# A long convolution with a feed-forward layer: another order of issue, block 3's feed-forward part in halves, and loads moved to GpSimd

## The chip, the cores and the metric

One core of one Trainium2 chip. The metric is the time of one execution on the device in microseconds; several executions are measured and their median is given. A core has five engines with instruction streams of their own: TensorE (PE in the profile; its weight loads are shown apart as PEld), VectorE (DVE), ScalarE (ACT), GpSimd (POOL) and SyncE (SP). Transfers are issued by SP or by GpSimd and carried out by the core's 16 DMA engines.

## The reference

Two layers on a sequence of 2048 tokens with 640 features, in bfloat16: a gated long convolution, then a SwiGLU feed-forward part with 1728 inner features. Cut to what matters:

```python
def reference(q, k, v, shift_k, ssm_k, ssm_D, w_gate, w_up, w_down):
    x = q
    # A: short causal convolution of k (4 taps), times v, then a causal
    # convolution over the whole sequence with the filter ssm_k, by FFT
    k_shift = sum(k_pad[:, t:t+S] * shift_k[:, 3 - t] for t in range(4))
    kv = k_shift * v
    y = irfft(rfft(kv, 2*S) * rfft(ssm_k, 2*S))[:S] + kv * ssm_D
    h = x + layernorm(x) * y
    # B
    n = layernorm(h)
    return h + (silu(n @ w_gate) * (n @ w_up)) @ w_down
```

## The kernel before

The sequence is cut into four blocks of 512 tokens, a block into four rows of 128 tokens. Everything is done on blocks: the spectrum of a block of the filter (G0 to G3), of a block of kv (X0 to X3), products of spectra added up over the blocks so far (the *mac* of block j has j + 1 pairs), the inverse transform, the gating, and the feed-forward part of the block. A transform is matrix products with constant matrices, WF forward and WI back, with DVE sums and differences around them.

- Loads: `load_k` (L477), the filter blocks g (`load_g`, L289), v (`load_t`, L296), x (`load_x`, L301), WF (L903), WI (L909), the row of ssm_D (L904, "skip"), the weights gate and up in three pieces each (`load_weights`, L737, into `wgu`) and down (`load_wd`, L746 and L749, into `wd`).
- Of block 0, k and g are turned by PE transposes (L411, with their eviction in L413), the later blocks by transposing DMAs (L404). The four taps are a matrix product (L490); DVE multiplies by v (L513 for block 0, with the kv in L515 for the later ones). Nine matrix products on the identity (L882, `warm`) stand between.
- Forward transforms: L329 on PE, evicted in L319 or L322. The mac: L537, L542 and L545 on DVE, and L581 and L582 at its end. The first normalisation is `ln1` (L606 to L636; its power on GpSimd, L610). The inverse transform: L662 to L677 on DVE, L698 on PE, L707 and L709. `turn_h` (L722 on ACT or L724 on DVE) normalises h and transposes it to hT.
- `ffn`: gate and up projections (`proj`, L769) in seven groups of 256 inner features; silu in L783, then either a copy of up by ACT and a DVE product (L785, L787) or one DVE product straight from PSUM (L786). The last 192 features stand apart (`odd_chunks`, L809 to L811, with the weights in `wodd`). Down projection: L833 and L845. The result of blocks 0 to 2 is put on top of h, which `ffn` has stored (L754), by an adding transfer on GpSimd (L852); block 3 adds on DVE (L862, L864).

`LEAD` gives for a block how many groups of `ffn` are done in halves of 256 tokens (`HALVES`: the rows 1, 3 first, then 0, 2), with a `matmul` of 256 columns in place of 512; a group that is not is done whole, after them.

No scheduler works here. Each piece of work is recorded with the buffers it reads and writes (`Plan.add`) and gets a number; `Plan.run` then emits the pieces in the order of the table `ORDER`, and every engine runs its own in that sequence. A number written as its complement (-20 for piece 19) takes the piece in its other form:

```python
for i in ORDER:
    op = self.ops[max(i, ~i)]
    assert op.deps <= done
    if i < 0:
        op.fn = op.other[2]
```

The other form of a load is the same load issued by GpSimd instead of SP; of an addition in the mac (`added`, L243) an adding transfer issued by GpSimd instead of a DVE instruction; of an eviction the DVE instead of ACT; of `turn_h` the DVE instead of ACT; of the up copy the single DVE product:

```python
def load(nbytes, fn, w, r=()):
    return plan.add("sp", nbytes, lambda: fn(nc.sync), r, w, ("pq", nbytes, lambda: fn(nc.gpsimd)))
```

Large tiles share an arena of 22 units, handed out in the same order ("arena" in the profile).

Of the kernel before, what the change touches and what calls it, by code (L numbers as in the profile page):

```python
# [41 lines left out]
LEAD = {0: 6, 3: 2}  # L42
# [149 lines left out]
def kernel(ctx: ExitStack, tc: tile.TileContext, A_q, A_k, A_v, A_shift_k, A_ssm_k, A_ssm_D, B_x,  # L192
# [458 lines left out]
    def inverse(A, x, n1, j, pieces=WHOLE):  # L651
# [50 lines left out]
        stats = []  # L702
        for rs in HALVES if LEAD.get(j) else (ROWS,):
            s = new("sm")
# [46 lines left out]
    def ffn(j, hT, h, n1, end=False):  # L751
# [6 lines left out]

        lead = LEAD.get(j, 0)

# [230 lines left out]
```

## Time and profile before

| | before |
|---|---|
| median of three executions | 251.34 us (250.96 to 253.92) |
| span of the profiled execution (no other time is recorded for it) | 251.4 us |
| PE busy | 237.3 us (94%) |
| PEld busy | 153.0 us (61%) |
| DVE busy | 197.7 us (79%) |
| ACT busy | 173.9 us (69%) |
| POOL busy | 54.0 us (21%) |
| moved by the DMA engines | 33.66 MB |

Busy times are those of one profiled execution. Weight loads run beside matrix products, so PE and PEld are not to be added. L numbers are lines of the kernel. A group row has the line, engine, operation, output and input tiles with their shapes and the count; then busy time and mean duration in ns; then the idle time ahead of them and what ended it. A timeline row has the start, the length and then the same, with the idle time before it in brackets. A row of transfers gives their count, the size of one and the median time from issue to landing. "SPq" and "POOLq" are the queues of transfers that these engines issue.

### The profile page before, as it was taken

The page shows a single profiled execution, that of the slowest core. Times are in us where ns is not written, and L with a number is a line of the kernel's source. Part 1 is how long each engine was busy: PE and PEld are TensorE (multiplying, and loading weights), DVE is VectorE, ACT ScalarE, POOL GpSimd, SP SyncE. Part 2 cuts the span into 40 slices and gives each one's busy share as a digit, 9 for nine tenths or more (in the row PEclk, how much of TensorE's full clock was granted, in tenths as well). Part 3 has the DMA queues.
Part 4 walks back from the last instruction along what each step waited for, and adds up shares of the span by engine and source line. Part 5 has one row for each costly group of instructions (what it writes and reads, how often), then busy time and mean ns, then how long its engine had stood idle before and what let it go on. Part 6 is the DMA issues. An engine that isn't in the chain of part 4 may idle for free.

```text
span 251.4 us, 5138 instructions
## 1 busy us (share of the span) xinstructions
PE 237.3 (94%) x2113; PEld 153.0 (61%) x2125; DVE 197.7 (79%) x249; ACT 173.9 (69%) x300; POOL 54.0 (21%) x54
## 2 busy tenths in 40 slices
PE   3869997999999999999999999999999999999994
PEld 3447675788777677444465676454456785465662
DVE  2379999999999999999999989999999542131222
ACT  2449998999999976975988789983542865325100
POOL 0002003231540313220270404263612110000030
PEclk9999999999999999999999999999999999999999
DMA  5995699774998654685345468889592200000052
GB/s 156 376 212 163 127 324 352 231 197 92 165 246 292 202 81 81 105 154 133 79 66 146 86 99 194 148 146 163 98 224 29 26 0 3 0 0 3 0 78 78
DMA packets 37283, 33.66 MB, mean 134 GB/s; under 512 B 22470, under 2 KB 32076, under 8 KB 37260
## 3 DMA queue, kind: packets, MB, share of 16 engines
q1 hardware_dynamic: 31884, 21.38, 32.1%
q0 software_dynamic: 5376, 11.96, 25.9%
q8 instruction: 16, 0.26, 0.4%
q14 instruction: 7, 0.06, 0.1%
HBM read 16.29 MB, written 4.59 MB: 83 GB/s over the span
## 4 chain that ended last, share of the span: by engine, by line
PE 56%; ACT 17%; DMA 10%; DVE 9%; issue 4%; SPq 3%; DVEq 0%; ACTq 0%; POOLq 0%
PE ps L769 24%; PE ps L845 22%; ACT arena L319 7%; DMA arena<-in_A_ssm_k_dram 7%; PE ps L698 5%; DMA arena<-arena 3%; ACT sg L785 2%; PE ps L490 2%; SPq L404 2%; ACT junk L606 1%; PE ps L329 1%; PE ps L833 1%; DVE arena L674 1%; DVE arena L663 1%; DVE arena L662 1%
## 5 line engine op out<-in xcount | busy, mean ns | idle before, releaser
L769 PE MATMUL ps<-arena,wgu 128*128 128x512 bf16 (+1 forms) x668 | 116.7, 328 | 1.4 <-ACT sg L809 0.5
L769 PEld LDWEIGHTS <-wgu 128*128 128x128 bf16 x680 | 66.2, 98 | 45.3 <-issue 1.4
L845 PE MATMUL ps<-wd,tT 128*128 128x320 bf16 x416 | 59.1, 299 | 0.0
L845 PEld LDWEIGHTS <-tT 128*128 128x128 bf16 x416 | 39.8, 98 | 17.2 <-issue 1.8
L542 DVE TENSOR_TENSOR arena<-arena 128x2560 bf16<-128x2560 bf16 x30 | 44.1, 1484 | 0.2
L783 ACT ACTIVATE sg<-ps 128x1024 bf16<-128x1024 f32 (+1 forms) x28 | 26.9, 968 | 20.3 <-PE ps L769 19.7
L329 PE MATMUL ps<-arena,WF 128*128 128x320 bf16 x176 | 29.8, 299 | 1.2 <-ACT arena L319 0.9
L785 ACT CAST sg<-ps 128x1024 bf16<-128x1024 f32 (+1 forms) x23 | 23.0, 998 | 6.9 <-PE ps L769 3.1
L319 ACT CAST arena<-ps 128x320 bf16<-128x320 f32 (+1 forms) x48 | 25.2, 583 | 1.9 <-DVE arena L545 1.1
L610 POOL TENSOR_TENSOR sm<-sm,neghalf 128x4 f32<-128x4 f32 (+1 forms) x10 | 16.6, 1659 | 43.4 <-DVE sm L646 43.1
L787 DVE TENSOR_TENSOR tT<-sg,sg 128x1024 bf16<-128x1024 bf16 (+1 forms) x23 | 15.5, 673 | 11.5 <-ACT sg L785 11.5
L243 POOL DMA_DIRECT2D arena<-arena x11 | 13.3, 1211 | 47.4 <-DVE arena L542 11.2
L329 PEld LDWEIGHTS <-WF 128*128 128x128 bf16 x176 | 17.1, 98 | 10.0 <-issue 2.3
L606 ACT ACTIVATE junk<-arena 128x640 bf16<-128x640 bf16 x28 | 20.8, 744 | 1.3 <-DVE arena L709 1.3
L545 DVE TENSOR_TENSOR arena<-arena 128x2560 bf16<-128x2560 bf16 x14 | 20.7, 1487 | 0.2
L319 ACT ACTIVATE arena<-ps 128x640 bf16<-128x640 f32 (+1 forms) x32 | 20.2, 655 | 0.3
L698 PE MATMUL ps<-arena,WI 128*128 128x320 bf16 x96 | 15.7, 299 | 0.9 <-issue 0.6
L850 ACT ACTIVATE row<-ps,sm 128x640 bf16<-128x640 f32 x12 | 9.5, 791 | 8.2 <-PE ps L845 8.0
L709 DVE SCALAR_TENSOR_TENSOR arena<-arena,sm,ps 128x640 bf16<-128x640 bf16 x16 | 13.6, 876 | 1.8 <-ACT ps L707 1.8
L852 POOL DMA_DIRECT2D out_dram<-row x12 | 11.7, 1153 | 14.1 <-ACT row L850 14.1
L707 ACT ACTIVATE ps<-ps,sm 128x640 f32<-128x640 f32 x16 | 12.1, 770 | 3.7 <-PE ps L698 3.5
L698 PEld LDWEIGHTS <-WI 128*128 128x128 bf16 x96 | 9.0, 97 | 5.6 <-issue 1.3
(91 smaller groups left out, 240.8 us busy)
## 6 DMA issues: line engine op xcount, KB each, us to landing
arena<-arena POOLq DMA_DIRECT2D x11, 640.0 KB, 6.1
arena<-in_A_q_dram SPq DMA_DIRECT2D x4, 640.0 KB, 5.1
out_dram<-row POOLq DMA_DIRECT2D x13, 160.0 KB, 4.2
arena<-in_A_ssm_k_dram SPq DMA_DIRECT2D x3, 640.0 KB, 9.4
arena<-in_A_v_dram SPq DMA_DIRECT2D x3, 640.0 KB, 6.3
wd<-in_B_w_down_dram SPq DMA_DIRECT2D x2, 800.0 KB, 7.3
out_dram<-arena POOLq DMA_DIRECT2D x2, 640.0 KB, 5.8
wgu<-in_B_w_gate_dram SPq DMA_DIRECT2D x1, 800.0 KB, 6.5
```

What stands on the lines that cost most here:

```text
L319: (lambda: nc.scalar.activation(dst(), src(), ACT.Copy, scale=2.0)) if twice else (lambda: nc.scalar.copy(dst(), src())),
L329: nc.tensor.matmul(ap(ps)[:, h, 0:NH], w, ap(src)[:, r, h * NH:(h + 1) * NH], start=(first and i == 0), stop=(last and i == len(rs) - 1), ...
L542: dve(1402, lambda: v.tensor_mul(to(), X.part(xs), H.part(hs)), [X.at(xs), H.at(hs)], [at])
L545: added(1402 * n - 69 * (n - 1), lambda: v.tensor_add(to(), to(), b()), to, b, [what], at, n)
L606: act(725, lambda r=r: nc.scalar.activation(waste(), ap(x)[:, r, :], ACT.Square, scale=D ** -0.5, accum_out=sm(s, MSQ, (r,))), [(x, r)], [ ...
L610: nc.gpsimd.tensor_tensor(sm(s, RSTD, rs), sm(s, VAR, rs), ap(neghalf)[:, 0:len(rs)], op=ALU.pow)
L698: nc.tensor.matmul(ap(ps)[:, w, 0:NH], m, src[:, w * NH:(w + 1) * NH], start=(i == 0), stop=(i == len(terms) - 1))
L769: nc.tensor.matmul(split(ap(ps), n)[:, i, :], w(k), ap(hT)[:, k, lo:lo + n], start=(k == 0), stop=(k == KT - 1))
L783: act(905 if wide_ else 490, lambda: nc.scalar.activation(of(sg), of(*gate), ACT.Silu), [(gate[0], gate[1] + i) for i in range(m)] + (psu ...
L785: op = plan.add("act", 905 if wide_ else 490, lambda: nc.scalar.copy(of(co), of(*up)), psu + [sg], [co] + tt, ("dve", 1135 if wide_ else 6 ...
L787: op.rest = dve(602 if wide_ else 336, lambda: nc.vector.tensor_mul(to(), of(sg), of(co)), [sg, co], tt)
L845: nc.tensor.matmul(ap(ps[hf])[:, hf, 0:NH], ap(tT)[:, c * BLK + at:c * BLK + at + P], ap(wd)[:, c, hf * NH:(hf + 1) * NH], start=False, st ...
```

## The change

`LEAD` for block 3 goes from 2 to 4, and `ORDER` is another table; all else is the same. Of the table the pieces that take their other form differ: 24 loads and stores are issued by GpSimd in place of 5, 13 additions of the mac go as adding transfers in place of 11 (with the 12 of `ffn` 25 in place of 23), seven up copies are joined with the product in DVE in place of five, and seven `turn_h` are on DVE in place of six.

```diff
-LEAD = {0: 6, 3: 2}
+LEAD = {0: 6, 3: 4}
...
 ORDER = (
-    0, 1, 2, 3, 16, 18, -20, 5, 4, 8, 17, 186, 9, 20, 22, 7, 10, 11, -22, 24, -26, 23, 26, 75, 76, 13, 15, 12, 6,
...
+    -27, -187, 16, 1, 8, 2, 5, 0, 3, 20, 18, 21, 7, 9, 19, 10, 11, 17, -16, 24, 22, -24, 25, 75, 76, 77, 6, -13, 78,
...
```

SP's program began with these rows: k in two parts, the taps, then g1, v0, WF, skip, g0 and the rest (`in_A_ssm_k` is the filter g, `in_A_q` is x):

```order
L477 DMA arena<-in_A_k_dram 128x1280
L889 DMA arena<-in_A_shift_k_dram 5x512
L477 DMA arena<-in_A_k_dram 128x1280
L289 DMA arena<-in_A_ssm_k_dram 128x5x512
L296 DMA arena<-in_A_v_dram 128x2560
L903 DMA WF<-const_wf 128x1024
L904 DMA arena<-in_A_ssm_D_dram 1x640
L289 DMA arena<-in_A_ssm_k_dram 128x5x512
L903 DMA WF<-const_wf 128x1024
L301 DMA arena<-in_A_q_dram 128x2560
```

Now SP has k, the taps and k, and then the x of block 1; GpSimd's program begins with these rows, where the mask for the identity (L872) used to stand alone:

```order
L296 DMA arena<-in_A_v_dram 128x2560
L289 DMA arena<-in_A_ssm_k_dram 128x5x512
L872 ISA
L872 AFFINE_SELECT ident<-ident 128x128
L904 DMA arena<-in_A_ssm_D_dram 1x16x40
L289 DMA arena<-in_A_ssm_k_dram 128x5x512
L903 DMA WF<-const_wf 128x1024 x2
L301 DMA arena<-in_A_q_dram 128x2560
L749 DMA wd<-in_B_w_down_dram 64x640
L909 DMA WI<-const_wi 128x1024 x2
```

So nine loads that SP issued at the start (v0, g1, skip, g0, x0, two each of WF and WI) and one tail of wd come from GpSimd's queue, with g1 and v0 ahead of g0 as before.

The second place is GpSimd's program around block 3's mac. Before, adding transfers of the mac stood between loads, powers and adding transfers of rows:

```order
L243 DMA arena<-arena 128x2x1280
L610 TENSOR_TENSOR sm_82<-sm_82,neghalf 128x2
L296 DMA arena<-in_A_v_dram 128x2560
L243 DMA arena<-arena 128x2x1280 x3
L634 TENSOR_TENSOR sm_83<-sm_83 128x4
L635 TENSOR_TENSOR sm_83<-sm_83 128x4
L636 TENSOR_SCALAR sm_83<-sm_83 128x4
L610 TENSOR_TENSOR sm_83<-sm_83,neghalf 128x4
L243 DMA arena<-arena 128x2x1280 x2
L852 DMA out_dram<-row_68 128x640
L243 DMA arena<-arena 128x2x1280
```

Now seven of them stand in one run, and the powers of `ln1` behind it:

```order
L243 DMA arena<-arena 128x2x1280
L610 TENSOR_TENSOR sm_82<-sm_82,neghalf 128x2
L852 DMA out_dram<-row_66 128x640
L852 DMA out_dram<-row_68 128x640
L852 DMA out_dram<-row_65 128x640
L243 DMA arena<-arena 128x2x1280 x7
L634 TENSOR_TENSOR sm_83<-sm_83 128x4
L635 TENSOR_TENSOR sm_83<-sm_83 128x4
L636 TENSOR_SCALAR sm_83<-sm_83 128x4
L610 TENSOR_TENSOR sm_83<-sm_83,neghalf 128x4
```

The load of block 3's v has gone from here to SP's queue, and the pieces 684, 691, 692 and 699 among the seven add to one accumulator.

The third place is DVE's program at the end of that mac, up to its closing steps L581 and L582 and the inverse transform (L662). Before:

```order
L390 TENSOR_TENSOR arena<-arena 128x2560
L393 TENSOR_TENSOR arena<-arena 128x2560
L542 TENSOR_TENSOR arena<-arena 128x2560 x2
L545 TENSOR_TENSOR arena<-arena 128x2x1280
L787 TENSOR_TENSOR tT<-sg_69,sg_70 128x1024
L542 TENSOR_TENSOR arena<-arena 128x2560
L787 TENSOR_TENSOR tT<-sg_71,sg_69 128x1024
L542 TENSOR_TENSOR arena<-arena 128x2560
L787 TENSOR_TENSOR tT<-sg_70,sg_71 128x1024
L545 TENSOR_TENSOR arena<-arena 128x2560
L581 TENSOR_TENSOR arena<-arena 128x2x1280
```

And now:

```order
L390 TENSOR_TENSOR arena<-arena 128x2560
L393 TENSOR_TENSOR arena<-arena 128x2560
L542 TENSOR_TENSOR arena<-arena 128x2560
L787 TENSOR_TENSOR tT<-sg_71,sg_70 128x1024
L542 TENSOR_TENSOR arena<-arena 128x2560 x3
L786 TENSOR_TENSOR tT<-sg_71,ps_72 128x1024
L545 TENSOR_TENSOR arena<-arena 128x2x1280
L787 TENSOR_TENSOR tT<-sg_69,sg_71 128x1024
L581 TENSOR_TENSOR arena<-arena 128x2x1280
L787 TENSOR_TENSOR tT<-sg_70,sg_69 128x1024
L582 TENSOR_TENSOR arena<-arena 128x2x1280
```

One addition (L545) is left between the products and L581 where there were two, one product of `ffn` is taken straight from PSUM (L786), and L582 is closer behind the last product of the mac.

82 rows, old and new, of the table ORDER are left out of this document.

## The prediction

> **What bounds the kernel now.** I read the windows first, because one average over the span hides that the stages have different limits. The rows give a stretch, its length, and the busy time of PE, weight loads, DVE, ACT and POOL.
>
> ```profile
> core 0: us, PE busy (x) PEld busy (x) DVE busy (x) ACT busy (x) POOL busy (x), PEclk, DMA share, GB/s
> 0.00:15.00 15.00, 7.93 (x174) 5.25 (x175) 5.80 (x16) 4.68 (x4) 0.54 (x6) 1.00 0.94 281
> 15.00:38.00 23.00, 22.84 (x287) 16.17 (x290) 21.88 (x41) 21.69 (x53) 1.88 (x2) 1.00 0.78 192
> 38.00:46.00 8.00, 6.15 (x74) 4.16 (x67) 7.79 (x14) 7.07 (x15) 2.04 (x1) 1.00 1.09 352
> 46.00:72.00 26.00, 25.41 (x228) 21.68 (x227) 25.05 (x25) 25.91 (x45) 10.71 (x8) 1.00 0.71 162
> 72.00:195.00 123.00, 122.19 (x1005) 71.73 (x1011) 120.18 (x123) 93.66 (x156) 34.74 (x33) 1.00 0.66 137
> 195.00:248.00 53.00, 52.79 (x365) 34.06 (x365) 16.46 (x34) 20.90 (x31) 4.04 (x6) 1.00 0.11 21
> ```
>
> From 15 us to 248 us PE is busy for 229.4 of 233 us, so nothing but less PE work or fewer PE gaps can shorten that part, and 3.6 us is all that gaps hold there. The first 15 us are another matter: PE works 7.9 us of them, and the DMA engines are at 0.94. The waits of PE and the chain name what it waits for (in the chain: start, length, what).
>
> ```profile
> PE ps L411 <- DMA arena<-in_A_k_dram: 4.0, 1, 4.0
> PE ps L411 <- DMA arena<-in_A_ssm_k_dram: 3.0, 1, 3.0
> ...
> PE ps L769 <- ACT sg L809: 0.5, 1, 0.5
> ```
>
> ```profile
> 3.90 11.01 DMA arena<-in_A_ssm_k_dram
> ...
> 14.96 1.03 PE ps L411 x15
> ```
>
> So of 251.4 us, 4.0 are the wait for the first k, 3.0 the wait for g0 (block 0 of the long filter, 640 KB) and everything behind is a PE-bound pipeline. From 15 to 195 us DVE is nearly as full (174.9 of 180 us by four of the windows), so a late DVE turns into a PE gap there; the last 53 us have DVE at 16.5 and are PE's alone.
>
> **The change part by part: the loads at the start.** This is the main term. Now the loads are issued by SP one behind another, and PE does this meanwhile:
>
> ```profile
> 2.52 0.52 SPq L296 DMA_DIRECT2D arena<-in_A_v_dram  x1
> 3.09 0.43 SPq L903 DMA_DIRECT2D WF<-const_wf  x1
> ...
> 3.90 0.38 SPq L289 DMA_DIRECT2D arena<-in_A_ssm_k_dram  x1
> ```
>
> ```profile
> 6.58 2.44 PE L490 MATMUL ps<-diag,kT 32*128 32x128 bf16 x112
> 8.95 2.68 PE L882 MATMUL ps<-ident 128*128 128x512 bf16 x9
> 11.55 0.43 PE L490 MATMUL ps<-diag,kT 32*128 32x128 bf16 x28
> 14.96 1.03 PE L411 MATMUL ps<-ident,arena 128*128 128x128 bf16 x15 [2.98 <-DMA arena<-in_A_ssm_k_dram]
> 15.82 0.82 PE L329 MATMUL ps<-arena,WF 128*128 128x320 bf16 x4
> ```
>
> ```profile
> 11.13 3.15 DVE L513 TENSOR_TENSOR arena<-ps,arena 128x512 bf16<-128x512 f32 x6 [3.83 <-DMA arena<-in_A_v_dram]
> ```
>
> After it, v0, g1, the skip row, g0, both halves of WF, x0, a tail of wd and WI go on GpSimd's queue from its first microsecond, with only the two halves of k0 and the taps left ahead on SP. Before, g0 took 11.0 us from issue to landing. What a load on GpSimd's queue takes is shown by two later ones, beside SP's medians for the same tensors (columns: count, size, median us to landing):
>
> ```profile
> 111.68 0.93 POOL L289 DMA_DIRECT2D arena<-in_A_ssm_k_dram  x1 [5.06 <-DMA arena<-arena]
> ...
> 151.73 0.62 POOL L296 DMA_DIRECT2D arena<-in_A_v_dram  x1 [6.59 <-DVE arena L542]
> ```
>
> ```profile
> arena<-in_A_ssm_k_dram SPq DMA_DIRECT2D x3, 640.0 KB, 9.4
> arena<-in_A_v_dram SPq DMA_DIRECT2D x3, 640.0 KB, 6.3
> ...
> arena<-in_A_ssm_k_dram POOLq DMA_DIRECT2D x1, 640.0 KB, 5.7
> arena<-in_A_v_dram POOLq DMA_DIRECT2D x1, 640.0 KB, 4.5
> ```
>
> Issue: v0 0.62, g1 0.93, the mask for the identity and the skip row some 1.2 together (estimate, as two loads of this kind), so g0 is issued at about 3.3 to 4.2 us, no earlier than now. What gets it in sooner is what travels beside it. Before, g1, v0 and WF (0.26 MB a half) were ahead on one queue, and the transfer moved far below the best rate. Ahead of or beside g0 are now k0, v0, g1 and g0 itself: 4 x 0.655 = 2.6 MB. At the 376 GB/s of the best slice
>
> ```profile
> GB/s 156 376 212 163 127 324 352 231 197 92 165 246 292 202 81 81 105 154 133 79 66 146 86 99 194 148 146 163 98 224 29 26 0 3 0 0 3 0 78 78
> ```
>
> that is 7.0 us from the first issue at 0.8 to 2 us: 8 to 9 us; with 5.7 us from an issue at 4.2 it is 9.9 us, with half of the WF bytes in front 11. All of it lies before 11.98 us, where PE's warm-up matmuls and the last taps end. PE then goes on without the 2.98 us wait; so the gain is bounded by 2.98 us at that place, whatever the landing. The other limb that leads to 15.82 us is DVE's six kv multiplications (3.15 us), now waiting for v0 till 11.13: with v0 there by about 6 us, they start when the taps are in PSUM at 8.9 and end at 12.1 to 12.6; PE would come to L329 at 11.98 + 0.86 = 12.8. That limb is done too. k0's second half shares its time with two more loads, which I take as 0 to 0.4 us late. Value: **-3.0 us**, bounds 0 (g0 lands at 14.9 as now) and -3.2.
>
> **The other moved loads.** The FFN weights (gate, up) go from SP to GpSimd's queue, behind v1 and g2. Block 0's FFN starts here:
>
> ```profile
> 45.23 2.89 PE L769 MATMUL ps<-arena,wgu 128*128 128x256 bf16 x25 [0.16 <-ACT arena L413]
> ```
>
> It must start at 42.2 for the gain to survive. v1 waits for a buffer that is free about 3 us earlier as well, and v1, g2 and the weights needed first are 3.6 MB, issued from 25 to 33 us; at the 352 GB/s of the 38 to 46 us window they take 10.2 us: landed by 39 to 40, a margin of some 2 us. If that cover is gone, each microsecond costs PE the same. I take 0, bounds 0 and +2.8 (rival three). The wait of v1 for its buffer now stands on GpSimd; queued behind it are g2, the weights, and block 0's L610, which the second normalisation needs near 40 us, some 7 us after the last of these issues, so that it is not late by this. GpSimd's own load rises by 19 issues of 0.6 to 0.9 us, 15 us on 54 of 251: no bound. In return SP gets v3 and the store of h2 (0.5 us each, as L296 above) and loses 21 others; its transposes stand behind fewer loads, which I cost at 0. In the 38 to 46 us window PE lacks 1.85 us; loads earlier by 3 us could take some of it: 0 to -1.
>
> **Block 3's FFN in halves.** Lead 4 instead of 2 turns 40 matmuls of 512 columns into 80 of 256. Their cadence is in the chain:
>
> ```profile
> 170.11 10.14 PE ps L769 x47
> ...
> 203.04 3.27 PE ps L769 x30
> ```
>
> 10.14 / 47 = 0.216 us and 3.27 / 30 = 0.109 us: 40 x 0.216 = 8.63 against 80 x 0.109 = 8.72, **+0.1 us**. The weight loads double, at 98 ns each, under the 109 ns of a matmul. The second half's hT comes later behind 8.7 us of PE work instead of 4.4, but nothing waited there that this could remove: that stretch has 52.79 of 53 us.
>
> **Two more adding transfers and the alternates.** Each of the two takes a DVE addition (1.484 us) off, so -2.97 us; three more wide L786 at 1.222 in place of L787 at 0.685 bring +1.61, and off ACT one copy each. The remaining exchanges (two k evictions and one of hT to ACT, one turn_h and one L322 to DVE, each 0.4 to 0.9 us) come to about -0.5 together: DVE -1.8 us, in all.
>
> ```profile
> L542 DVE TENSOR_TENSOR arena<-arena 128x2560 bf16<-128x2560 bf16 x30 | 44.1, 1484 | 0.2
> ...
> L787 DVE TENSOR_TENSOR tT<-sg,sg 128x1024 bf16<-128x1024 bf16 x22 | 15.1, 685 | 11.5 <-ACT sg L785 11.5
> ...
> L786 DVE TENSOR_TENSOR tT<-sg,ps 128x1024 bf16<-128x1024 bf16 x2 | 2.4, 1222 | 6.2 <-PE ps L769 6.2
> ```
>
> DVE is the second bound from 15 to 195 us, but PE's gaps there are 3.6 us, of which most are short pieces at other waits, so I credit **-0.4 us** for this and the 38 to 46 us window together, bounds +0.5 and -2.5. The tail is the same code.
>
> **Sum**, against the profiled span, 251.4, which is the median (251.34) but for 0.1: 251.4 - 3.0 + 0.1 - 0.4 = 248.1, say **248.0 us**. A difference under 2% (246.3 to 256.4) is about what a measurement of this kernel cannot tell from none.
>
> [...] The trace: g-loads landed 9.4 us after issue on SP (median of three) and 5.7 on GpSimd, at different times with different company. [...]
>
> **The rivals.**
> 1. *The start gains next to nothing.* The bytes that now precede g0 are the same but for one half of WF: 0.26 MB / 376 GB/s = 0.7 us. For it: 0.94 busy. Against it: slices of 163 and 127 GB/s that follow 376 (a slice is 6.3 us), so the bytes were not the limit, and the 5.7 against 9.4 us. Time: 251.4 - 0.7 = **250.7**. Chance 0.2.
> 2. *Slower: block 3's adding chain.* After the change GpSimd has seven adding transfers in a row, and four of them (ops 684, 691, 692, 699) add to the same accumulator, each waiting till the last has landed, where DVE needs the fourth at its closing step L582. The rows of now:
>
> ```profile
> 158.86 1.48 DVE L515 TENSOR_TENSOR arena<-arena 128x2560 bf16<-128x2560 bf16 x1
> ...
> 187.54 1.48 DVE L582 TENSOR_TENSOR arena<-arena 128x2560 bf16<-128x2560 bf16 x1
> ```
>
> ```profile
> arena<-arena POOLq DMA_DIRECT2D x11, 640.0 KB, 6.1
> ```
>
> DVE has 29.8 us of its own work from the issue of 684 to that step (its rows' durations in the new order; the like stretch is 30.2 us now, from 158.86 to the end of the last row); three transfers of 6.1 end at 18.3, the fourth is issued only at 22.7, behind another on the queue whose DVE input is late, and lands at 28.8: margin 1.0. Once 4 T exceeds 29.8, T over 7.45 us, each microsecond of T costs four. Behind L582 stand the inverse transform and PE's L698, which now starts with no slack (PE busy 122.19 of 123). At T = 9.4, the slowest 640 KB row above, the delay is 37.6 - 29.8 = 7.8: 248.0 + 7.8 = **255.8**; at T = 8.5 it is 252.2. For it: more bytes are in flight at once; against it: the DMA share there is 0.66, and eleven transfers have a median of 6.1. Chance 0.1.
> 3. *GpSimd cannot write its loads in time.* 24 loads at up to one DVE instruction each: if an issue waits for a running 1.48 us DVE operation, five issues ahead of the weights take 5 x (1.48 - 0.93) = 2.8 us more: 248.0 + 2.8 = **250.8**. Against it: 0.93 and 0.62 us issues with DVE 97% busy. Chance 0.1. [...]
> 4. *More of the gaps close.* If DVE's 1.8 us and the 1.85 us of the window from 38 to 46 come in at 2.5 together instead of 0.4: **245.9**. Chance 0.2.
>
> **How the numbers follow.** The forecast (247.0 to 249.5) has 0.4. Range 245.0 to 252.3: from rival four at its full bounds (251.4 - 3.2 - 2.5 - 0.7 for short gaps) to rivals one and three, and to rival two at T = 8.5; what is beyond is some 0.15. Faster by over 2%, below 246.3, is most of rival four and a little of the forecast: 0.25; slower than 256.4 is rival two at T above 9.5 or two mishaps at once: 0.08; the rest, 0.67, is within 2%.
>
> **What would show it.** In the profile after: the 3.0 us wait of PE for the filter gone or under 0.5, and the first L329 near 12.8; v0 landed before 9 (DVE's L513 starts near 8.9); the first L769 near 42; 40 fewer L769 of 512 columns and 80 more of 256 (but for lost records); GpSimd issues under 1.3 us; the last of the seven transfers landed about 1 us ahead of L582; PE's busy time still near 237.4. I am wrong if g0 lands at 14 or later in the company of the same bytes, if the weights land after 42, or if DVE has an idle piece before L582.

## The result, and the profile after

| | before | after |
|---|---|---|
| median of 13 executions each | 251.6 us (250.69 to 254.52) | 254.08 us (252.55 to 255.35) |
| after / before, with 95% interval | | 1.0091 [1.0068, 1.0115] |
| profiled execution: time, span | not recorded, 251.4 us | 255.09 us, 253.4 us |
| PE, DVE, ACT, POOL busy | 237.3, 197.7, 173.9, 54.0 us | 238.4, 195.8, 171.7, 73.2 us |

The change made the kernel about 1% slower. The prediction was 248.0 us, with a range of 245.0 to 252.3: the sign was wrong and the time lies outside the range, though inside the 2% that one measurement cannot tell from no change. Two further series of after, beside other series of before, came to 1.0029 [0.9994, 1.0063] and 1.0037 [1.0004, 1.0070], so the loss is between nothing and 1%, and a gain is excluded or nearly so. Ratios and intervals leave disturbed executions out; medians are of all.

I begin with the waits of PE in the profile after (total us, number, longest), because the prediction's main term was a wait that should go.

```profile
PE ps L411 <- DMA arena<-in_A_k_dram: 7.4, 2, 4.0
PE ps L329 <- ACT arena L319: 1.1, 2, 0.7
PE ps L698 <- issue: 0.9, 1, 0.9
PE ps L411 <- DVE row L724: 0.4, 1, 0.4
```

The wait for the filter (3.0 before) is gone, as predicted. But the wait for k, 4.0 once, is now 7.4 in two. The timeline of PE's start (start, length, what, and in brackets the idle time ahead with its releaser) shows where the second one stands:

```profile
4.04 1.25 PE L411 MATMUL ps<-ident,arena 128*128 128x128 bf16 x10 [4.04 <-DMA arena<-in_A_k_dram]
5.22 0.29 PE L894 MATMUL ps<-ident,arena 5*128 5x5 bf16 x4
8.86 1.25 PE L411 MATMUL ps<-ident,arena 128*128 128x128 bf16 x10 [3.34 <-DMA arena<-in_A_k_dram]
...
10.76 1.71 PE L490 MATMUL ps<-diag,kT 32*128 32x64 bf16 x104 [0.35 <-DVE kT L413]
12.40 3.24 PE L882 MATMUL ps<-ident 128*128 128x512 bf16 x9
15.58 0.43 PE L490 MATMUL ps<-diag,kT 32*128 32x128 bf16 x28
15.94 1.12 PE L411 MATMUL ps<-ident,arena 128*128 128x128 bf16 x15
16.95 0.43 PE L329 MATMUL ps<-arena,WF 128*128 128x320 bf16 x2
```

PE has turned half of k0 and stands still for 3.34 us until the other half has landed; everything behind moves with it, the warm-up included, and the first L329 comes at 16.95 where it came at 15.82. The chain of work, which began with g0's 11.01 us, now begins with k0's second half, 7.15 us on its way (start, length, what):

```profile
1.66 7.15 DMA arena<-in_A_k_dram
10.76 1.71 PE ps L490 x86
```

The transfers say the same: the first row is that of the profile before, the second of the profile after (count, size, median us to landing).

```profile
arena<-in_A_k_dram SPq DMA_DIRECT2D x2, 320.0 KB, 3.1
```

```profile
arena<-in_A_k_dram SPq DMA_DIRECT2D x2, 320.0 KB, 5.2
```

The windows after have the prediction's stretches, with the last one to 250 (length, then busy us of PE, PEld, DVE, ACT, POOL, granted clock, DMA share, GB/s):

```profile
0.00:15.00 15.00, 7.26 (x143) 4.83 (x144) 4.54 (x12) 5.96 (x6) 6.90 (x16) 1.00 0.86 298
15.00:38.00 23.00, 22.77 (x301) 16.02 (x300) 21.47 (x42) 21.09 (x52) 8.19 (x8) 1.00 0.75 198
38.00:46.00 8.00, 5.59 (x65) 3.37 (x64) 6.92 (x15) 6.77 (x16) 3.09 (x3) 1.00 1.03 353
46.00:72.00 26.00, 25.51 (x232) 21.86 (x232) 25.39 (x24) 25.44 (x43) 10.71 (x6) 1.00 0.88 196
72.00:195.00 123.00, 122.52 (x1013) 71.87 (x1011) 119.61 (x124) 90.24 (x153) 38.20 (x36) 1.00 0.69 135
195.00:250.00 55.00, 54.74 (x419) 39.17 (x417) 17.57 (x34) 22.18 (x33) 6.09 (x8) 1.00 0.14 23
```

PE does 0.67 us less in the first 15 us and 0.56 less from 38 to 46 than before; from 72 us on it is about as full as it was (122.52 of 123 and 54.74 of 55). The first two GpSimd rows at work, from its timeline, are the competitors of k0's second half:

```profile
1.33 0.69 POOL L296 DMA_DIRECT2D arena<-in_A_v_dram  x1 [0.83 <-POOLq L975]
2.03 0.90 POOL L289 DMA_DIRECT2D arena<-in_A_ssm_k_dram  x1
```

v0 is issued at 1.33, ahead of k0's second half (1.66), and g1 right behind it. Before, both stood behind k0 on SP's own queue. By these issues and the times to landing, v0 (7.7 us) was there at 9.0 and g0 (issued at 3.84, 8.7 us) at 12.5: g0 did come sooner than the 14.9 of before, though not by the 8 to 11 that the prediction had.

### The profile page after: what moved, and what is told of

Same layout as the page of the kernel before. It is cut to its first block, busy times and chain, and to the rows that moved or that the text cites. A ratio compares the mean times of both kernels' runs of the same rounds, so it can differ in the third digit from the quotient of the medians.

```text
span 253.4 us, 5240 instructions
## 1 busy us (share of the span) xinstructions
PE 238.4 (94%) x2165; PEld 157.1 (62%) x2165; DVE 195.8 (77%) x246; ACT 171.7 (68%) x299; POOL 73.2 (29%) x75
## 4 chain that ended last, share of the span: by engine, by line
PE 51%; DVE 26%; DMA 9%; ACT 6%; issue 5%; POOL 1%; SPq 0%; DVEq 0%; POOLq 0%; ACTq 0%
PE ps L769 21%; PE ps L845 17%; DVE arena L542 7%; ACT arena L319 4%; PE ps L698 4%; DMA arena<-in_A_k_dram 3%; PE ps L329 3%; DVE arena L545 3%; DVE tT L787 2%; DMA arena<-arena 2%; DMA arena<-in_A_v_dram 2%; DVE arena L709 2%; PE ps L490 2%; DMA out_dram<-row 2%; PE ps L411 1%
## 5 line engine op out<-in xcount | busy, mean ns | idle before, releaser
L769 PE MATMUL ps<-arena,wgu 128*128 128x256 bf16 (+1 forms) x720 | 116.9, 320 | 0.2 <-ACT arena L413 0.2
L769 PEld LDWEIGHTS <-wgu 128*128 128x128 bf16 x720 | 70.1, 98 | 41.3 <-issue 0.7
L542 DVE TENSOR_TENSOR arena<-arena 128x2560 bf16<-128x2560 bf16 x30 | 43.8, 1486 | 0.1
L329 PE MATMUL ps<-arena,WF 128*128 128x320 bf16 x176 | 29.1, 299 | 1.3 <-ACT arena L319 1.1
L785 ACT CAST sg<-ps 128x1024 bf16<-128x1024 f32 (+1 forms) x21 | 20.5, 978 | 10.9 <-DVE tT L786 5.4
L610 POOL TENSOR_TENSOR sm<-sm,neghalf 128x4 f32<-128x4 f32 (+1 forms) x10 | 20.1, 2013 | 22.6 <-DVE sm L646 22.2
L243 POOL DMA_DIRECT2D arena<-arena x13 | 15.7, 1248 | 36.2 <-DVE arena L542 20.3
L319 ACT CAST arena<-ps 128x320 bf16<-128x320 f32 (+1 forms) x48 | 24.7, 593 | 0.2
L329 PEld LDWEIGHTS <-WF 128*128 128x128 bf16 x176 | 17.1, 98 | 9.6 <-issue 2.1
L787 DVE TENSOR_TENSOR tT<-sg,sg 128x1024 bf16<-128x1024 bf16 (+1 forms) x21 | 13.9, 661 | 10.0 <-ACT sg L785 10.0
L852 POOL DMA_DIRECT2D out_dram<-row x12 | 11.7, 1026 | 29.1 <-ACT row L850 29.0
L319 ACT ACTIVATE arena<-ps 128x640 bf16<-128x640 f32 (+1 forms) x31 | 18.8, 652 | 1.6 <-PE ps L329 1.3
L545 DVE TENSOR_TENSOR arena<-arena 128x2560 bf16<-128x2560 bf16 x12 | 17.9, 1488 | 0.2
L698 PE MATMUL ps<-arena,WI 128*128 128x320 bf16 x96 | 15.6, 299 | 1.0 <-issue 0.9
L709 DVE SCALAR_TENSOR_TENSOR arena<-arena,sm,ps 128x640 bf16<-128x640 bf16 x16 | 13.6, 877 | 2.4 <-ACT ps L707 2.4
L786 DVE TENSOR_TENSOR tT<-sg,ps 128x1024 bf16<-128x1024 bf16 (+1 forms) x7 | 7.4, 1068 | 9.2 <-ACT sg L783 5.1
```

The lines of the kernel that those rows point to most:

```text
L319: (lambda: nc.scalar.activation(dst(), src(), ACT.Copy, scale=2.0)) if twice else (lambda: nc.scalar.copy(dst(), src())),
L329: nc.tensor.matmul(ap(ps)[:, h, 0:NH], w, ap(src)[:, r, h * NH:(h + 1) * NH], start=(first and i == 0), stop=(last and i == len(rs) - 1), ...
L542: dve(1402, lambda: v.tensor_mul(to(), X.part(xs), H.part(hs)), [X.at(xs), H.at(hs)], [at])
L545: added(1402 * n - 69 * (n - 1), lambda: v.tensor_add(to(), to(), b()), to, b, [what], at, n)
L610: nc.gpsimd.tensor_tensor(sm(s, RSTD, rs), sm(s, VAR, rs), ap(neghalf)[:, 0:len(rs)], op=ALU.pow)
L698: nc.tensor.matmul(ap(ps)[:, w, 0:NH], m, src[:, w * NH:(w + 1) * NH], start=(i == 0), stop=(i == len(terms) - 1))
```

## The experiments

Theory A: the start loses by sharing what it gains by queueing earlier: v0 and g1, in flight on GpSimd's queue, delay k0's second half, and one wait takes the place of the other. Theory B: the loss lies in the later order (block 0's FFN, whose first L769 comes at 47.83 in place of 45.23), the start being neutral. Theory C, added later: whatever is done at the start, the last of its loads decides. Each expectation below uses letters of its own for its rivals; theories A to C in this text are the three named here. In the diffs 16 and 17 are the halves of k0, 8 the taps, 26 is v0, 186 g1, 12 g0, 13 and 14 WF, 15 the skip row, 27 x0; -27 is v0 by GpSimd.

The experiments on the start are read by one table. From the start of the first L329 to the start of PE's last instruction the length is 231.0 to 233.4 us in all rows but h4's, so the first L329 is most of what the start costs. An execution's time is 1.7 us over its span (after: 255.09 and 253.4). The figures of e3 and of f2 to f4 stand with these runs.

| profiled execution | wait for k0's 2nd half | wait for g0 | first L329 at | from there to the start of PE's last | its time |
|---|---|---|---|---|---|
| before, first profile | 0 | 2.98 | 15.82 | 231.8 | (span 251.4) |
| before, b3 | 0 | 2.02 | 14.72 | 232.3 | 252.46 |
| before, f1 | 0 | 3.98 | 16.64 | 232.2 | 254.33 |
| before, b4 | 0 | 3.84 | 16.46 | 233.4 | 255.31 |
| after, first profile | 3.34 | 0 | 16.95 | 232.5 | 255.09 |
| after, a2 | 1.60 | 0 | 14.06 | 231.6 | 251.29 |
| after, a3 | 1.43 | 0 | 14.79 | 231.0 | 251.48 |
| m1, start of after | 3.04 | 0 | 16.87 | 232.5 | 255.03 |
| e1, start's loads back on SP | 0 | 0.47, and 3.06 for v0 | 18.18 | 232.9 | 256.96 |
| e2, v0 and g1 alone moved | 3.27 | 0 | 16.27 | 231.6 | 252.99 |
| e4, GpSimd's loads held | 0 | 2.21 | 16.44 | 232.4 | 254.57 |
| h4, v0 and g1 held | 0 | 0, and 4.69 for v0 | 18.54 | 235.5 | 259.16 |
| h5b, g1 and g0 held | 0.31 | 4.83 | 18.35 | 232.3 | 255.76 |
| p1, k0 on the same queue | 0 | 0 | 14.08 | 232.0 | 251.86 |
| n1, v0 on SP, rest held | 0.31 | 0 | 13.70 | 232.5 | 251.89 |

**e1: the start's loads back on SP**, the rest of after kept.

```diff
-    -27, -187, 16, 1, 8, 2, 5, 0, 3, 20, 18, 21, 7, 9, 19, 10, 11, 17, -16, 24, 22, -24,
+    16, 1, 8, 2, 5, 0, 3, 20, 18, 21, 7, 9, 19, 10, 11, 17, 186, 26, 13, 15, 12, 14, 24, 22, -24,
...
-    34, -14, 196, 35, 38, -40, 40, 92, -15, 194, -42, -28,
+    34, 35, 38, -40, 40, 92, -42, 27, 196, 192, 194,
```

> The changed kernel with the loads of the start (g1, v0, WF, skip, g0, x0) back on SP's queue behind k0, in the order of before; WI and the tail of wd stay on GpSimd. Theory A (the loads on GpSimd's queue share the DMA engines with the second half of k0 and hold it up by 4 us, and the start is lost by this): the second wait of PE for k0 goes, the first L329 is back at 15.8 us from 16.95, and the time falls by 1.1 us, to about 253.0; the remaining 1.4 us over before lie elsewhere. Rival B (the start is no part of it, the loss is in the body): no change, 253.8 to 254.3.

Measured: 255.72 us, 1.0131 [1.0087, 1.0176]. k0 is in time again, but v0 is now late, and PE waits for the DVE products (L513) that need it. The timeline of PE:

```profile
15.51 0.61 PE L490 MATMUL ps<-diag,kT 32*128 32x128 bf16 x26 [3.06 <-DVE arena L513]
```

A's wait vanished as expected, and both numbers of the expectation were missed. The start is not quite that of before: WI and a tail of wd stay on GpSimd's queue, where they are issued from 1.49 to 3.3 us, and so they go beside v0. Issued at 2.52 as in before, v0 took 11.5 us to land in place of 8.5, and g0, issued at 3.90 in both, 12.7 in place of 11.0. The same kind of sharing has moved to other loads.

**e2: before, with only v0 and g1 moved** to the head of GpSimd's program.

```diff
-    0, 1, 2, 3, 16, 18, -20, 5, 4, 8, 17, 186, 9, 20, 22, 7, 10, 11, -22, 24, -26, 23, 26,
+    -27, -187, 0, 1, 2, 3, 16, 18, -20, 5, 4, 8, 17, 9, 20, 22, 7, 10, 11, -22, 24, -26, 23,
```

> The kernel of before with only v0 and g1 moved to the head of GpSimd's queue, everything else as before. Theory A: the second half of k0 lands at 8 to 9 us instead of under 5, PE gets a second wait for it of about 3 us, the warm-up comes after 12 us, and the first L329 is at 16.5 to 17 instead of 15.82: 0.7 to 1.2 us slower than before, 252.3 to 252.8. Rival B: k0 unaffected, v0 earlier, no change or a small gain: 251.0 to 251.6.

Measured: 252.82 us, 1.0002 [0.9965, 1.0039]. The timeline of PE in e2, where 8.69 is k0's second half and 15.24 is g0's transposes, now without a wait:

```profile
4.70 0.71 PE L411 MATMUL ps<-ident,arena 128*128 128x128 bf16 x5
8.69 1.25 PE L411 MATMUL ps<-ident,arena 128*128 128x128 bf16 x10 [3.27 <-DMA arena<-in_A_k_dram]
9.86 2.31 PE L490 MATMUL ps<-diag,kT 32*128 32x128 bf16 x112
12.11 2.84 PE L882 MATMUL ps<-ident 128*128 128x512 bf16 x9
14.88 0.43 PE L490 MATMUL ps<-diag,kT 32*128 32x128 bf16 x28
15.24 1.15 PE L411 MATMUL ps<-ident,arena 128*128 128x128 bf16 x15
```

This is the plainest run of the study: two loads moved, nothing else, and the 3.0 us wait for g0 is exchanged for 3.27 us for k0, with the time unchanged. Theory A's wait and time came as expected; its first L329 came at 16.27, a little early.

**e3: after without the warm-up products** (they are no part of the result).

```diff
-WARM = 9
+WARM = 0
```

> The changed kernel without the nine warm-up matmuls (L882), which are no part of the result. Theory A, with a second part: since k0 is late, the 3.24 us of the warm-up stand on the path between the taps and the last taps and g0's turn; without them the first L329 comes 1.5 to 3 us earlier, less what PE loses at a slower rate, 251.4 to 253. Rival C: g0, WF or v0 is not there before 15.9 us anyway, so that the wait only changes its name: 253.8 to 254.3, with a PE wait for the filter or for DVE in place of L882.

Measured: 254.15 us, 1.0067 [1.0033, 1.0102]. Rival C of this expectation came true, its theory A did not: where the warm-up stood, PE now waits for the products with v0.

```profile
13.42 0.61 PE L490 MATMUL ps<-diag,kT 32*128 32x128 bf16 x26 [1.33 <-DVE arena L513]
```

The first L329 comes 1.3 us earlier (15.63) than in the first profile of after; 0.5 of it is k0's second half, whose transposes start at 8.38 here and at 8.86 there. g0's transposes take 1.88 in place of 1.12 us, and from the first L329 on it is 233.2 in place of 232.5. Without the warm-up nothing is gained.

**e4: all GpSimd loads of the start held until k0 has landed.** A copy of one column by GpSimd, which waits for k0, stands ahead of them (piece 931); its result is overwritten.

```diff
-    -27, -187, 16, 1, 8, 2, 5, 0, 3, 20, 18,
+    0, 3, 16, 8, 17, 931, -27, -187, 1, 2, 5, 20, 18,
...
+    plan.add("pool", 100, lambda: nc.gpsimd.tensor_copy(ap(neghalf)[:, 0:1], rd(held[0])[:, 3, 0:1]), [(held[0], 1)], [])
```

> The changed kernel with all its GpSimd loads held back until k0 has landed: GpSimd first does the identity's mask, then copies one column of k0's second half into a constant that is overwritten later (so it waits for that load), and then issues v0, g1, skip, g0 and so on in the order of the change. Theory A: k0's second half lands at about 5 us as before, v0 at about 8 to 9, g0 by about 12, the first L329 at 12.8 to 13.8 instead of 16.95: 250.0 to 251.2. Rival C: the 2.6 MB need the same time whatever their order, so g0 lands as late as 14 to 15 and L329 is at 15 to 16: 252 to 253.

Measured: 255.56 us, 1.0128 [1.0088, 1.0168]. k0's wait is gone, so the loads beside it are its cause; but now g0 is issued at 7.00 and PE waits for it again:

```profile
5.33 1.25 PE L411 MATMUL ps<-ident,arena 128*128 128x128 bf16 x10
...
15.00 1.64 PE L411 MATMUL ps<-ident,arena 128*128 128x128 bf16 x15 [2.21 <-DMA arena<-in_A_ssm_k_dram]
```

The expectation had k0 right and g0 not: it was to land by 12 us and did at 15.0, so both of its times were missed.

**f2, f3, f4: hybrids of the two orders**, to put B to the test: f2 has the first 62 entries of before's table and then after's, f3 the first 75 of after's and then before's, f4 the first 400 of before's and then after's. Each has the pieces that the head lacks behind it; in f3 WI is issued by SP.

> The first 62 entries of the order of before, and then the rest of the changed order: the loads of the start on SP and PE's order at the start as before, everything behind as changed (LEAD 4, the other loads on GpSimd, the adds). Theory A2 (of the 2.4 us that the change costs, some 1.6 are the start and 0.8 the body): 252.0 to 252.6. Rival B (all in the body): 253.5 to 254.2. Rival C (all in the start): 251.3 to 251.9.

> The mirror: the first 75 entries of the changed order (its start), then the rest of the order of before, with LEAD 2. The two halves of WI go on SP here. Theory A2: first L329 at 16.5 to 17, k0's second half late, 252.9 to 253.5. Rival B: 251.3 to 251.9. Rival C: 253.8 to 254.3.

> The first 400 entries of the order of before (up to about 80 us of its trace, loads included), then the rest of the changed order with LEAD 4, the adding transfers of blocks 2 and 3 and the loads of that part on GpSimd. Theory A3 (the body's loss lies before 80 us, the rest of the change costs nothing or gains 0.3): ratio to before 0.998 to 1.002. Rival F (halves, adds and loads of the later part cost it): 1.006 to 1.010.

Measured: 254.51, 255.42 and 255.02 us; 1.0100 [1.0044, 1.0156], 1.0118 [1.0047, 1.0188], 1.0105 [1.0074, 1.0136]. These do not decide. f3 has waits of its own, 1.9 us at L698, and from first L329 to the end it has 234.5; f4 has 0.8 at L329 and 235.7: at the seam the hybrids stall where neither parent does. f2 (first L329 at 16.42, then 233.0) would fit B, but its start is not that of before either: WI and the tail of wd go on GpSimd's queue from 1.47 us, k0's second half is 0.63 us late, PE waits 3.23 for g0, and its granted clock is 0.84 from 15 to 18 us. f4's ratio lies just above the range of rival F, but with these stalls it is no evidence for it.

**f1, b3, b4: before, profiled again**, one execution each.

> The kernel of before, once more, for a second profile. Executions of it last 251.6 us in the median and 249.9 by span, while the one profiled first had a span of 251.4: it was slower than the median by about 1.5 us. Theory A (what varies is when g0 has landed): here the first L329 starts earlier than 15.82, at 14 to 15, with the rest of the span, from there to the last matmul, the same 231.8. Rival B (what varies is the body): the first L329 again at about 15.8 and the difference behind it.

> The kernel of before, one look. If its time is near the median of before, 251.3 to 252.3: theory A (what varies is when g0 lands): PE's wait for the filter 1.5 to 2.2 us instead of 3.0, first L329 at 14.2 to 15.0, and 231.5 to 232.0 from there to the last matmul. Rival B (the body varies): first L329 at 15.8, the body 230.5. If the clock drops, the wait is over 3 us and the time 254 to 255.

> The same once more, with the same expectations: first L329 and PE's wait for the filter move with the time, the body stays within 231.5 to 232.3.

Measured: 254.33, 252.46 and 255.31 us. The wait for g0 is 2.0 to 4.0 us from one execution to another of the same kernel. b3 came as expected; f1, expected at 14 to 15, has its first L329 at 16.64, and b4's 233.4 is above its 231.5 to 232.3. The row of b3, the execution that is nearest to the medians (251.6 to 252.7):

```profile
13.86 1.03 PE L411 MATMUL ps<-ident,arena 128*128 128x128 bf16 x15 [2.02 <-DMA arena<-in_A_ssm_k_dram]
14.72 0.82 PE L329 MATMUL ps<-arena,WF 128*128 128x320 bf16 x4
```

So the prediction's profile, with 2.98, showed an execution slower than most: its span of 251.4 plus 1.7 is about 253.1, an estimate, 1.5 over the median.

**a2, a3: after, again.**

> The changed kernel once more, on the chip and beside the runs of before that the next three are compared with. Expected ratio to before 1.007 to 1.011, first L329 at 15.9 to 17, with k0's second half late as before in its profile.

> The changed kernel as the reference for the three others on their chip: ratio to before 1.002 to 1.010, PE's second wait for k0 1.5 to 3.5 us, first L329 at 14 to 17.

Measured: 252.68 us, 1.0029 [0.9994, 1.0063], and 253.30 us, 1.0037 [1.0004, 1.0070]. a2 is below its expectation, and both profiled executions are the fastest of their series; in a3 PE's second wait for k0 is this:

```profile
6.86 1.25 PE L411 MATMUL ps<-ident,arena 128*128 128x128 bf16 x10 [1.43 <-DMA arena<-in_A_k_dram]
```

The whole difference to the first profile of after (3.6 us) is 2.2 at the first L329 and 1.5 behind it. From the first L329 on, after needs 231.0, 231.6 and 232.5 us, before 231.8, 232.2 and 232.3 (233.4 in b4): theory B, a loss in the later order, has no support in these rows. They are single executions: for the medians it is an inference.

**m1: after, with the turned rows of block 0 (pieces 149, 150, 161, 164) moved ahead**, since from 38 to 46 us PE waits for L724.

```diff
-    151, 152, 231, 149, 150, 232, 245, 246, 240, 241, 157, 233, -162, 234, 162, 163, 235, 236, -165,
+    151, 149, 150, -162, -165, 152, 231, 232, 245, 246, 240, 241, 157, 233, 234, 162, 163, 235, 236,
```

> The changed kernel with four pieces of block 0 moved in the order, L610 and L648 of the first two rows and their two turn_h rows (L724), ahead of the last L709 of that block, as they stand in the order of before. In the changed order DVE meets that L709 first, which waits 1.04 us for ACT, and the rows, on which PE's transposes wait, come at 44.6 us instead of 41.7. Theory D (this costs most of the body's loss between 38 and 48 us): 0.5 to 0.9 us faster than the changed kernel run beside it, and PE's wait for L724 gone. Rival E (ACT is the bound there, at 6.8 of 8 us busy): the wait only changes its name, 0 to 0.2 us.

Measured: 252.87 us, 1.0037 [1.0002, 1.0071], beside a2 no gain, as rival E had it. The wait for L724 is gone, the one for L319 has grown from 0.45 to 1.03, and L769 waits 1.0 for a transposing DMA of a row. Its start is that of after, and k0's second half is late by 3.04:

```profile
8.47 1.25 PE L411 MATMUL ps<-ident,arena 128*128 128x128 bf16 x10 [3.04 <-DMA arena<-in_A_k_dram]
...
45.74 0.70 PE L329 MATMUL ps<-arena,WF 128*128 128x320 bf16 x4 [1.03 <-ACT arena L319]
```

**p1: after, with both halves of k0 at the head of GpSimd's own queue**, so that v0 and g1 stand behind them.

```diff
-    -27, -187, 16, 1, 8, 2, 5, 0, 3, 20, 18, 21, 7, 9, 19, 10, 11, 17, -16,
+    0, -17, 8, -18, -27, -187, 3, 1, 2, 5, 20, 18, 21, 7, 9, 19, 10, 11, -16,
```

> The changed kernel with the two halves of k0 moved to the head of GpSimd's queue, ahead of v0 and g1, so that they stand in one queue. Theory A (loads in another queue share the DMA engines with k0's second half; behind it in its own queue they cannot): k0 is issued about 0.5 to 0.9 us later, but complete by 5.5 to 6, PE's second wait for it is under 1 us, g0 and WF are there by 13, first L329 at 13.5 to 14.5: ratio to before 0.995 to 1.000, and 0.5 to 2.5 us faster than the changed kernel beside it. Rival G (GpSimd's queue is slow by itself at the start): k0 at 7 or later, no gain over the changed kernel.

Measured: 252.22 us, 1.0012 [0.9983, 1.0041]; a3 beside it 253.30, with an interval that overlaps, so that here the rows show more than the time. The timeline of PE in p1:

```profile
4.75 1.25 PE L411 MATMUL ps<-ident,arena 128*128 128x128 bf16 x10 [4.75 <-DMA arena<-in_A_k_dram]
5.93 0.29 PE L894 MATMUL ps<-ident,arena 5*128 5x5 bf16 x4
6.15 1.25 PE L411 MATMUL ps<-ident,arena 128*128 128x128 bf16 x10
```

The same loads, the same bytes, and no second wait (1.43 us in a3 beside it): k0 was late because v0 and g1 went beside it and not behind it. GpSimd issues k0 at 1.33 us where SP had begun at 0.79, so the first half comes 0.7 us later, and that is the price of this version. The rows came as this expectation's theory A had them; the ratio is just above its 1.000.

**n1: after, with v0 on SP behind k0 and the GpSimd loads held until k0's first half has landed** (the gate of e4, reading the first half).

```diff
-    -27, -187, 16, 1, 8, 2, 5, 0, 3, 20, 18,
+    0, 3, 16, 8, 17, 26, 931, -187, 1, 2, 5, 20, 18,
...
+    plan.add("pool", 100, lambda: nc.gpsimd.tensor_copy(ap(neghalf)[:, 0:1], rd(held[0])[:, 1, 0:1]), [(held[0], 0)], [])
```

> The changed kernel with v0 on SP's queue right behind k0, and GpSimd's loads (g1, skip, g0, WF and so on) held until the first half of k0 has landed (GpSimd first copies one column of it into a constant that is overwritten later). Theory A: k0 by 5, v0 by 8 to 9, g1 by 9.5 to 10.5, g0 by 12 to 13, first L329 at 13.8 to 14.5 and no second wait for k0: ratio to before 0.995 to 1.002. Rival C (the sum of the bytes decides): g0 at 14 to 15.5, PE waits for it, its clock drops, ratio 1.005 to 1.015.

Measured: 251.48 us (250.42 to 251.92), 0.9977 [0.9952, 1.0002]: the fastest kernel of the study, 1.8 us under a3 beside it, and under before by an interval that just touches no change, as this expectation's theory A had it. k0's second half is 0.31 us late and no wait for g0 or v0 is left:

```profile
5.67 1.25 PE L411 MATMUL ps<-ident,arena 128*128 128x128 bf16 x10 [0.31 <-DMA arena<-in_A_k_dram]
...
13.70 0.43 PE L329 MATMUL ps<-arena,WF 128*128 128x320 bf16 x2
...
38.08 2.08 PE L698 MATMUL ps<-arena,WI 128*128 128x320 bf16 x14 [1.31 <-issue]
```

**h4 and h5b: before, with the same idea.** h4 puts v0 and g1 on GpSimd behind a gate on k0; h5b leaves v0 on SP and puts g1 and g0 on GpSimd behind a gate on k0's first half (923 is the gate).

```diff
-    0, 1, 2, 3, 16, 18, -20, 5, 4, 8, 17, 186, 9, 20, 22, 7, 10, 11, -22, 24, -26, 23, 26, 75, 76,
+    0, 1, 2, 3, 16, 18, -20, 5, 8, 17, 923, -27, -187, 4, 9, 20, 22, 7, 10, 11, -22, 24, -26, 23, 75, 76,
```

```diff
-    0, 1, 2, 3, 16, 18, -20, 5, 4, 8, 17, 186, 9, 20, 22, 7, 10, 11, -22, 24, -26, 23, 26, 75, 76, 13, 15, 12,
+    0, 1, 2, 3, 16, 18, -20, 5, 8, 17, 923, 4, -187, 9, 20, 22, 7, 10, 11, -22, 24, -26, 23, 26, 75, 76, 13, 15, -13,
```

> The kernel of before with v0 and g1 moved to GpSimd's queue, but held until k0 has landed (GpSimd first copies one column of k0's second half); g0, WF and the others move up on SP's queue right behind k0. If the order of the bytes is what decides (theory A): k0 by 5, v0 by 9, g0 by 10 to 11, no PE wait between the warm-up and g0's turn, first L329 at 12.8 to 13.8: 249.0 to 250.3. Rival C (the sum of the bytes decides): g0 at 13 to 15 as now, 251 to 252.

> The kernel of before with v0 right behind k0 on SP's queue, WF behind it, and g1 and g0 on GpSimd, held until the first half of k0 has landed (GpSimd first copies one column of it). Theory A: v0 by 8 to 9, g1 by 9 to 10, g0 by 11.5 to 12.5, PE's wait for the filter below 1 us and no drop of its clock, first L329 at 12.8 to 13.8: ratio 0.990 to 0.996. Rival C: g0 at 13 to 15, ratio 0.998 to 1.01.

Measured: 258.86 us, 1.0262 [1.0204, 1.0320], and 257.07 us, 1.0220 [1.0196, 1.0244]. Both expectations were missed by far. (h5, another table for the idea of h5b, has no time.) In h4 PE waits 4.2 us at once for DVE's L513, which has no v0; in h5b it waits for g0:

```profile
16.76 1.79 PE L411 MATMUL ps<-ident,arena 128*128 128x128 bf16 x15 [4.83 <-DMA arena<-in_A_ssm_k_dram]
```

Being held is only a part of it. v0 is issued at 4.84 in h4 and at 4.83 in e4; it takes 10.0 us in h4, with WF, g0, x0 and WI issued on SP's queue from 2.04 to 4.33, and at most 4.3 in e4 (L513 starts at 9.15 there, released by PE), where these stand behind it on its own queue. g0 takes 11.5 us from 5.23 in h5b, with x0 and WI on SP's queue, and 7.0 from 5.66 in n1, where they stand behind it. So theory C has to be read with what is on the other queue: of k0, v0 and g0 the one that lands latest for its place in PE's program is what PE waits for, and p1 and n1 are the only orders tried in which, behind k0's first half, PE waits for none of the three by more than 0.31 us.

## Why the prediction was wrong

**The step that failed** is "k0's second half shares its time with two more loads, which I take as 0 to 0.4 us late". It was 3.34 us late in the first profile after, 1.43 and 1.60 in two others, 3.27 in e2. Its landing is the first link of everything that follows, so the delay counts in full: the transposes, the taps, the nine warm-up products and the last taps come behind it, and g0, there at 12.5 and not turned before 15.94, no longer mattered. The prediction had worked out when the *late* load would come sooner and had not followed the *early* one, although the same two loads now went beside it.

**A second term** was mis-sized as well: g0 was to land at 8 to 11 us, in any case before 11.98, and landed at 12.5 in the first profile after (11.0 in a2, 11.7 in a3, 12.4 in p1, 12.7 in n1). Without any wait for k0 the first L329 of that profile would have been nearer 13.6 than 12.8, an estimate from 12.5 and the 1.0 us that lies between g0's transposes and the first L329 there.

**The size.** A wait of 2.0 to 4.0 us for g0 became one of 1.4 to 3.3 us for k0, and the first L329 moved from 14.7 to 16.6 (before) to 14.1 to 17.0 (after). The predicted 12.8 was reached by no version; n1 came to 13.70. There g0 lands at 12.7, as the last taps end, and the warm-up takes 3.18 us in place of the 2.68 that the sum had copied from before, and it begins at 9.21 in place of 8.95.

**The base.** "The profiled span, 251.4, which is the median (251.34) but for 0.1" set a span beside a time. An execution's time is 1.7 us above its span, so the profiled one was slower than the median, and part of the 2.98 us that was to go was not in the median execution at all: b3, near the medians, had 2.02. Even with k0 in time, the gain on the median would have been nearer 2 than 3.

**The argument against the main term** was the better one: rival one took the DMA engines' share of 0.94 in the first window as a sign that they were full, and gave the start 0.7 us. The runs show more than that: k0's second half took 7.15 us beside the other queue's loads, and 2.99 in e4, where these are held. I had put the full engines down as "no gain" (rival one, 250.7) and not as "the load ahead loses". One argument against it was a misreading: the slices of 163 and 127 GB/s lie at 18.9 to 31.4 us, after g0 had landed at 14.9; the slice of 376 is that from 6.3 to 12.6 us, while g0 was on its way.

**The other terms.**
- Weights: 0, in that no row shows PE waiting for `wgu`. But the margin of 2 us was not there: the five pieces on GpSimd's queue landed from 42.0 to 51.7 us (the first issued at 33.29 and 8.7 us on its way), where the prediction had 39 to 40 and named a landing after 42 as a sign of being wrong. The first L769 came at 47.83 against 45.23 in the profiles first compared, not at 42; whether the weights would have been in time for 42 is not shown. The later start is the first L329's 1.13 us and another 1.47 us between there and L769; by PE's last instruction the second part is down to 0.7 (232.5 against 231.8), and in a3 the same L769 starts at 44.75.
- Halves of block 3: +0.1, and no stall of this part shows. The rows are x320 of 512 columns and x400 of 256 after, where 40 fewer and 80 more were expected; before's x348 of 360 shows that records are missing there.

```profile
L769 PE MATMUL ps<-arena,wgu 128*128 128x512 bf16 x320 | 71.7, 379 | 0.0
L769 PE MATMUL ps<-arena,wgu 128*128 128x256 bf16 x400 | 46.7, 273 | 0.2 <-ACT arena L413 0.2
```

- DVE: busy 1.9 us less (predicted 1.8). As a gain of 0.4 it does not stand out from the 231.0 to 232.5 us that after needs behind the first L329.

**The rivals.** Rival one, no gain at the start, is nearest, though its cause was the bytes ahead of g0 and the cause shown is the delay of k0. Rival two, the adding chain, did not happen: the last of the seven was issued at 182.43, the thirteen have a median of 6.5 us, and DVE's closing steps follow without a wait. This one took 5.6 us and landed at 188.1, 0.8 us ahead of L582, where the prediction had about 1:

```profile
182.43 1.20 POOL L243 DMA_DIRECT2D arena<-arena  x1 [3.35 <-DVE arena L542]
...
186.83 1.49 DVE L581 TENSOR_TENSOR arena<-arena 128x2560 bf16<-128x2560 bf16 x1
188.23 0.69 DVE L787 TENSOR_TENSOR tT<-sg,sg 128x1024 bf16<-128x1024 bf16 x1
188.83 1.49 DVE L582 TENSOR_TENSOR arena<-arena 128x2560 bf16<-128x2560 bf16 x1
```

Rival three, slow issues, did not happen: the loads at the start took 0.69 and 0.90 us to issue, those of the weights about 0.86. Rival four, closing gaps: from 38 to 46 us PE had 5.59 us, less than the 6.15 of before.

**What stays open.** Why k0's second half is 1.4 us late in one execution of after and 3.3 in another, and whether the difference between the series (1.0091 and 1.003) is this delay alone. The four profiled executions with after's start, of 251.3, 251.5, 255.0 (m1) and 255.1 us, go with 1.60, 1.43, 3.04 and 3.34 us; m1 ran beside a2, so the delay changes from execution to execution. It is not the delay alone, either: of the 2.9 us between the first L329 of a2 and that of the first profile, 1.9 are k0's and 1.0 the warm-up's (last section). Why n1 waits 1.31 us ahead of L698 ("issue", no releaser in the trace), where b3 has 1.0 and the first profile of before 0.59, wasn't tried.

## What to carry to other kernels

When a load is moved to another engine's queue, write down which loads it used to stand behind: those were its competitors here, and the first of them on the critical path paid (k0's second half, 3.27 us late in e2). The same held for the loads that stayed on the other queue (PE waited 3.06 us for v0 in e1, 4.69 in h4). Follow each of the inputs that the first stage needs, not only the one that is late now, since the wait moved between them (3.27 us for k0 in e2, 3.06 and 4.69 for v0 in e1 and h4, 4.83 for g0 in h5b). And set a profiled span against the time of the same execution before taking it for the median.

## What the hardware showed

In some executions PE's granted clock fell in the middle of the start, to 0.60 in b4 and to 0.51 in f1 from 15 to 18 us, and the wait for a load then cost more than its length. The windows from 15 to 18 us, of b3 first and of b4 behind it, two executions of the same kernel (the column after the last count is the granted clock):

```profile
15.00:18.00 3.00, 3.00 (x27) 2.19 (x25) 2.84 (x10) 2.75 (x9) 0.00 (x0) 1.00 0.84 173
```

```profile
15.00:18.00 3.00, 2.81 (x24) 2.35 (x25) 1.18 (x3) 1.36 (x3) 0.00 (x0) 0.60 0.88 98
```

In b4 PE had waited 3.84 us for g0, in b3 2.02. g0's fifteen transposes took 1.48 us in b4 and 1.79 in f1 (wait 3.98, clock 0.51) where they took 1.03 in b3. Behind the 4.83 us of h5b the clock was 0.66 from 18 to 21 us. The runs also show the drop behind shorter waits, 2.21 us in e4 (clock 0.54) and 2.50 in f4 (0.58), and none behind 2.98 in the first profile of before (1.00); what decides between these was not tried. In the warm-up after, the first six products start 403 to 427 ns apart and the last three 216 or 217, although the profile's column for the granted clock reads 1.00 there. The nine took 3.24 us there and 2.26 in a2. This does not follow the wait ahead of them: they took 3.55 us in e4 with no second wait for k0 and 3.18 in n1 with 0.31, but 2.26 in a2 with 1.60 and 2.46 in f3 with 2.96. So the length of the warm-up moves the first L329 by up to 1.3 us from one execution with after's start to another (2.26 in a2, 3.54 in m1), and what sets it is not shown by these runs.
